# Key groups of one PSUM bank, query units over half a run, transposing transfers for four batches, and a new order of work

## The chip, the cores and the metric

The kernel runs on one core of one Trainium2 chip. The core has a matrix engine (TensorE, PE in the profile, with its weight loads listed as PEld), a vector engine (VectorE, DVE), an activation engine (ScalarE, ACT), a general engine (GpSimd, POOL) and a queue engine that mostly issues transfers (SyncE, SP). Each engine takes its instructions strictly in the order in which the program lists them; they meet only through semaphores. Matrix results land in PSUM, eight banks of 2 KB in each of 128 partitions, and everything else is in SBUF. The metric is device microseconds for one execution.

## The reference

Two layers for 8 batches of 576 tokens, 8 heads of 64: a linear attention with an exponential feature map, and behind it a causal gate of five taps around a linear unit.

```python
def phi(x):                                   # for q and for k
    proj = np.einsum('bhsd,df->bhsf', x, w_phi)          # 64 -> 128 features
    proj = proj - np.max(np.abs(proj), axis=-1, keepdims=True)
    return np.concatenate([np.exp(proj), np.exp(-proj)], axis=-1)
q_p, k_p = (phi(q), phi(k))
kv = np.einsum('bhsf,bhsd->bhfd', k_p, v)
z = np.sum(k_p, axis=2)
num = np.einsum('bhsf,bhfd->bhsd', q_p, kv)
den = np.einsum('bhsf,bhf->bhs', q_p, z)[..., None] + 1e-06
x = num / den                                 # heads joined: (8, 576, 512)
gate_pre[:, t] = sum(conv_w[m] * x[:, t - 4 + m] for m in range(5))
gate = 1.0 / (1.0 + np.exp(-gate_pre))
out = (gate * (x @ w_val)) @ w_out
```

The output is float32, 8 x 576 x 512. (The gate is computed as a tanh, with the halves folded into the taps and into the last scaling.)

## The kernel before

The eight batches run through one software pipeline. A batch has two tokens side by side in the 128 partitions (64 channels each), which gives 18 blocks of 128 columns; these are cut into five units (`UNITS`, four of four blocks and one of two).

For each batch, in the names that the code gives its tasks:

- **Loads.** k and q come from DRAM; for batch 0 as float32 in pieces on SP's queue (`load32`), turned by PE (`tp32`) and copied to bf16 by ACT or DVE (`tc32`); for batch 1 as bf16 by POOL's queue, turned by PE (`tp16`, `tc16`); from batch 2 on by POOL's queue and then turned by a transposing transfer on SP's queue (`xpose`). v comes in with `loadv`.
- **Keys.** `kp`: PE projects a unit into two banks, one for each of the two tokens. `kmax`: DVE takes the greatest magnitude over features out of both banks in one reduction. `kexp`: ACT takes the exponential of both banks, once for each sign. `ek` (ACT) makes the factors that undo the missing subtraction (exp of minus the maximum for one sign, of plus the maximum for the other), `vs` (POOL) multiplies them into v (tile VT), `st` (PE) sums keys times values, and `kv` (DVE or ACT) takes the sums out of PSUM.
- **Queries.** `qm`, `qmax`: the same projection and reduction. The maxima are turned (`mqt`, `mqr`) and spread over a diagonal by POOL (`rx`, tile RX); `qp` projects again in the other layout and subtracts the maxima by a second pair of matmuls against RX; `qexp` (ACT) writes the features into QTIL and, for the unit of two blocks, into QTT.
- **Attention out.** `num` (PE, five parts c = 0..4) waits in this version for every `qexp` of the batch; `nrm` (DVE) divides; the result is turned by PE and taken out of PSUM by DVE or ACT (`xtp`, `xtc`), or, for the batches in `XB`, turned by a transposing transfer on SP's queue (`xtd`).
- **Gate and output.** `gate` and `val` (PE), `tanh` (ACT), `gv` (DVE), `out` (PE), `oev` (ACT or DVE), and `odma`, the store on SP's queue.

The order of the work is written out in three tables. `build()` makes one list of tasks; `ORDER` is the sequence in which their instructions are put out, so that each engine's queue is the part of this sequence that belongs to it. `FLEX` gives an engine to each task that may run on two, and `BANKS` gives every group its PSUM banks. `WARM` and `ZERO` put further matmuls between the tasks, which add zeros to a bank (line 504) or are overwritten (line 491); the output doesn't depend on them. `hold` and `holdx` are tiny POOL copies that read a tile only so that POOL's queue of loads stands still until the tile has landed.

Of the kernel before, what the change touches and what calls it, by code (L numbers as in the profile page):

```python
# [27 lines left out]
XB = (6, 7)  # L28
# [6 lines left out]
WARM = (  # L35
    "60:6:1 81:1:1 87:7:2 134:7:1 141:7:1 "
)
ZERO = "35:76:7 61:80:5 75:34:1 101:105:1 118:99:1 126:215:8 144:223:1 155:192:4 158:200:1 175:315:6 189:346:1 195:241:2 197:241:2 211:327:1"
# [41 lines left out]
)  # L80
FLEX = (
    "AAAAAADAAADDPPPPDDDDAADDDDDDDDDDDDDAAADAAAADDDDAAADDDAADAAADDADAADDDDADDDDADDDDDDAADADDAAAAAA"
)
BANKS = (
    "037362307001454523232323016701676714232367230101676012354423010145454501013660564675601456745010145450101676767014501454"
# [77 lines left out]
def build(plan, em=None):  # L163
# [11 lines left out]
    def G(*k):  # L175
        return h.get(k)
# [724 lines left out]
```

## Time and profile before

| what | value |
|---|---|
| three timed runs | 218.59, 218.91, 219.14 us; median 218.91 us |
| span of the profiled execution, first to last instruction | 217.7 us |
| around the span (median less span; the page has no separate time for the profiled execution) | 1.2 us |
| PE busy | 195.5 us, 90% |
| ACT busy | 180.8 us, 83% |
| DVE busy | 170.2 us, 78% |
| POOL busy | 132.8 us, 61% |
| moved by DMA | 39.92 MB, 183 GB/s over the span |
| granted PE clock, mean | 0.995 |

The share of busy time of an engine is an average over the whole span, and this span has three parts: a start in which batch 0 has nothing beside it, a middle in which three batches overlap, and an end in which only the last gates and outputs are left. The table of stretches tells them apart. A row of instruction groups gives the busy time of the group, the mean of one instruction and the idle time in front of it; since consecutive instructions on ACT and DVE overlap by about a tenth of a microsecond, the busy time of a pair in the timeline is less than two means. PE's ends are modelled, and a matmul that waits inside the pipeline counts as busy.

### The profile page before, as it was taken

To read this page: it belongs to the slowest core of one execution; us is meant where nothing else is said; L and a number is where in the kernel's file an instruction comes from. 1 tells how busy PE (TensorE), PEld (TensorE's weight loads), DVE (VectorE), ACT (ScalarE), POOL (GpSimd) and SP (SyncE) were. 2 spreads that over 40 slices of the span, in tenths; PEclk is the share of its full clock that TensorE was granted. 3 is DMA by queue.
4 is the path that set the end of the run, shared out by engine and by line. 5 is a ranking of instruction groups with operands and counts; after the bars stand their busy time and mean duration, and the time that the engine had idled before them with its cause. 6 is when DMAs were issued, how large, how long until landed. Compare 5 with 4: busy or idle time off the path is not lost.

```text
span 217.7 us, 9029 instructions
## 1 busy us (share of the span) xinstructions
PE 195.5 (90%) x3946; PEld 138.6 (64%) x3946; DVE 170.2 (78%) x257; ACT 180.8 (83%) x267; POOL 132.8 (61%) x172
## 2 busy tenths in 40 slices
PE   2787887778999999998999999999999999899990
PEld 2555565566676676676857776567757766687740
DVE  3199979999789988997899978998699897654510
ACT  3589999999989899998999997999988988634251
POOL 3055999897793838970999089902993879210010
PEclk9999999999999999999999999999999999999997
DMA  6999998899899799989999778969953265764166
GB/s 177 364 234 215 302 188 231 149 174 199 144 152 284 139 135 213 302 154 174 233 276 168 88 165 248 190 142 203 287 183 89 63 160 128 81 168 97 48 186 202
DMA packets 49954, 39.92 MB, mean 183 GB/s; under 512 B 34165, under 2 KB 39541, under 8 KB 49914
## 3 DMA queue, kind: packets, MB, share of 16 engines
q1 hardware_dynamic: 43616, 28.65, 55.6%
q0 software_dynamic: 6032, 10.49, 26.3%
q8 instruction: 31, 0.51, 0.9%
q10 hardware_dynamic: 266, 0.21, 0.3%
q14 instruction: 9, 0.07, 0.1%
HBM read 30.48 MB, written 9.44 MB: 183 GB/s over the span
## 4 chain that ended last, share of the span: by engine, by line
PE 52%; ACT 23%; DVE 14%; DMA 5%; issue 4%; SPq 0%; DVEq 0%; ACTq 0%
PE PS L791 11%; ACT QTIL L706 9%; PE PS L781 9%; PE PS L813 9%; ACT KTIL L595 8%; DVE MQP L585 5%; PE PS L620 5%; PE PS L577 4%; PE PS L719 4%; DVE MK L585 3%; DMA KTIL<-in_k_dram 3%; PE PS L693 2%; DMA XT<-XN 2%; PE PS L817 2%; PE PS L698 2%
## 5 line engine op out<-in xcount | busy, mean ns | idle before, releaser
L595 ACT ACTIVATE KTIL<-PS 128x1024 bf16<-128x1024 f32 (+1 forms) x80 | 71.9, 960 | 4.1 <-PE PS L577 2.0
L610 POOL TENSOR_TENSOR VT<-VN,EK 128x1152 bf16<-128x1152 f32 x32 | 67.9, 2123 | 4.0 <-ACT EK L604 3.9
L706 ACT ACTIVATE QTIL<-PS 128x1024 bf16<-128x1024 f32 x64 | 62.5, 1044 | 2.4 <-PE PS L698 1.6
L682 POOL TENSOR_TENSOR RX<-MQR,ident 128x512 bf16<-128x512 bf16 (+1 forms) x39 | 36.6, 964 | 35.7 <-DVE MQR L670 26.0
L585 DVE TENSOR_REDUCE MK<-PS 128x8 f32<-128x1024 f32 (+1 forms) x40 | 44.2, 1112 | 2.9 <-PE PS L577 1.2
L585 DVE TENSOR_REDUCE MQP<-PS 128x8 bf16<-128x1024 f32 (+1 forms) x40 | 43.6, 1112 | 3.1 <-PE PS L577 2.3
L791 PE MATMUL PS<-XT,WV 128*128 128x288 bf16 x256 | 34.8, 286 | 0.3 <-DVE GV L797 0.2
L797 DVE SCALAR_TENSOR_TENSOR GV<-TH,PS 128x576 bf16<-128x576 bf16 x32 | 23.8, 752 | 10.4 <-PE PS L791 4.7
L813 PE MATMUL PS<-WOUT,GV 128*128 128x512 bf16 x128 | 31.3, 380 | 0.0
L791 PEld LDWEIGHTS <-WV 128*128 128x128 bf16 x256 | 23.8, 98 | 7.9 <-issue 1.4
L785 ACT ACTIVATE TH<-PS 128x576 bf16<-128x576 f32 x32 | 20.3, 663 | 9.5 <-PE PS L781 6.3
L620 PE MATMUL PS<-VT,KTIL 64*128 64x65 bf16 x1152 | 23.3, 191 | 1.1 <-issue 1.0
L781 PE MATMUL PS<-XT,GW 64*64 64x288 bf16 x640 | 23.1, 285 | 0.9 <-DMA XT<-XN 0.8
L740 DVE TENSOR_TENSOR XN<-PS,RCP 128x512 bf16<-128x512 f32 x32 | 22.1, 692 | 1.5 <-DMA XT<-XN 0.4
L620 PEld LDWEIGHTS <-KTIL 64*128 64x128 bf16 x1152 | 20.8, 94 | 3.8 <-issue 2.5
L719 PEld LDWEIGHTS <-QTIL 128*128 128x128 bf16 x512 | 18.3, 97 | 6.4 <-issue 4.0
L719 PE MATMUL PS<-KV,QTIL 128*128 128x65 bf16 x512 | 20.3, 194 | 0.3 <-DVE MQP L585 0.2
L781 PEld LDWEIGHTS <-GW 64*64 64x64 bf16 x640 | 17.8, 106 | 3.3 <-DVE RCP L737 0.9
L634 ACT ACTIVATE OUTS<-PS 128x512 f32<-128x512 f32 x22 | 13.5, 619 | 7.3 <-PE PS L813 6.1
L577 PE MATMUL PS<-W,qT 64*128 64x128 bf16 x288 | 15.1, 217 | 3.7 <-ACT qT L544 0.9
L813 PEld LDWEIGHTS <-GV 128*128 128x128 bf16 x128 | 11.1, 98 | 11.3 <-issue 0.6
L577 PEld LDWEIGHTS <-qT 64*128 64x128 bf16 x288 | 10.6, 94 | 10.3 <-issue 5.2
(79 smaller groups left out, 235.6 us busy)
## 6 DMA issues: line engine op xcount, KB each, us to landing
out_dram<-OUTS SPq DMA_DIRECT2D x32, 256.0 KB, 3.4
VN<-in_v_dram SPq DMA_DIRECT2D x7, 1152.0 KB, 6.3
KQN<-in_q_dram POOLq DMA_DIRECT2D x6, 576.0 KB, 8.3
KQN<-in_k_dram POOLq DMA_DIRECT2D x6, 576.0 KB, 9.8
KTIL<-in_k_dram SPq DMA_DIRECT2D x4, 288.0 KB, 4.5
VN<-in_v_dram POOLq DMA_DIRECT2D x1, 1152.0 KB, 10.6
KTIL<-in_q_dram SPq DMA_DIRECT2D x4, 256.0 KB, 5.7
out_dram<-OUTS SPq DMA_DIRECT2D x14, 64.0 KB, 2.6
```

The source lines that it names most:

```text
L577: nc.tensor.matmul(self.PS[:, t.grp.banks[par], i * P:(i + 1) * P], X[rows, (c0 + i) * P:(c0 + i + 1) * P], self.W2[rows, :], start=True, ...
L585: self.nc.vector.tensor_reduce(o, self.two(t.grp, n * P).rearrange("p a (c f) -> p a c f", f=F), AX.X, ALU.max, apply_absolute_value=True)
L595: self.nc.scalar.activation(self.KTIL[b % 2][:, s, c0:c0 + n, :, :].rearrange("p c a f -> p a c f"), self.two(t.grp, n * P).rearrange("p a ...
L610: nc.gpsimd.tensor_tensor(self.VT[g][:, s, :, 0:D], self.VN[b % 2][:, NC * g:NC * g + NC, :], e.to_broadcast([P, NC, D]), ALU.mult)
L620: nc.tensor.matmul(self.PS[:, t.grp.banks[ab], (s * 2 + x) * E1:(s * 2 + x + 1) * E1], self.KTIL[b % 2][rows, s, J // 2, J % 2, :], self.V ...
L682: self.nc.gpsimd.tensor_tensor(o, *wide(self.MQR[self.mq(b, u)][:, :], self.ident2), ALU.mult)
L706: self.nc.scalar.activation(o, i, AF.Exp, scale=1.0 - 2.0 * s)
L719: nc.tensor.matmul(self.PS[:, t.grp.banks[h // 4], (h % 4) * E1:(h % 4 + 1) * E1], Q[:, s, c % 2, h, (c // 2) * P:(c // 2 + 1) * P], self. ...
L781: self.nc.tensor.matmul(self.PS[o * D:(o + 1) * D, t.grp.banks[par], 0:R], self.GW[r, jj, 4 - m, :], X[r, 4 * a + jj, :, HALO - 8 * s:HALO ...
L791: self.nc.tensor.matmul(self.PS[:, t.grp.banks[par], 0:R], self.WV[:, i, (2 * j + par) * D:(2 * j + par + 2) * D], X[:, 4 * par + i, :, HA ...
L797: nc.vector.scalar_tensor_tensor(out=self.GV[b % 3][:, j, :, :], in0=self.TH[j][:, :, :], scalar=1.0, in1=self.two(t.grp, R), op0=ALU.add, ...
L813: nc.tensor.matmul(self.PS[:, t.grp.banks[0], :], GV[:, j, c % 2, (c // 2) * XH:(c // 2) * XH + P], self.WOUT[:, j, c % 2, :], start=(j == ...
```

## The change

Six things change, and the three tables with them.

1. **Key units.** A key unit still has one projection, but its two banks are two groups of their own (`gs`), each with its own reduction (`kmax`, one bank) and its own two exponentials (`kexp`, one bank). On DVE 40 reductions become 80 of half the size, on ACT 80 exponentials become 160 of half the size.
2. **Query units.** Units 0 to 3 no longer hold four blocks of all 16 runs of 8 tokens, but half of them (`qys`, `k=2`): units 0 and 1 make up one half of the columns of QTIL, units 2 and 3 the other. `num` for c = 0, 1 waits for units 0 and 1 alone, c = 2, 3 for units 2 and 3, c = 4 for unit 4. The second operand of `qp` is now contiguous (`RX[u][rows, 0:w]`). A unit needs two blocks of the turned input (`QNEED`), and in batch 0, whose maxima are turned in two parts, units 0 and 2 follow the first and the others the second (`QOF`).
3. **Transposing transfers.** `XB` grows from batches 6, 7 to 4, 5, 6, 7: 32 PE transposes and four copies out of PSUM go, and four transposing transfers of 256 KB come in on SP's queue.
4. **Engines.** `vs` and `rx` may run on DVE as well as on POOL. In the table, one of 32 `vs` and four of 40 `rx` are on DVE (one `rx` before). Of the copies, KV goes from 12 on DVE and 4 on ACT to 8 and 8, the output from 14 and 22 to 19 and 17.
5. **Filling matmuls.** `ZERO` is empty: the 152 matmuls against zeros go. `WARM` has one entry of two, against six matmuls in five entries.
6. **First loads.** The last piece of q is loaded first, `w_phi` comes in one transfer, `conv_w` moves from ACT's queue to SP's behind the pieces of k and q, and POOL's queue is held until all pieces of batch 0 have landed; batch 1 loads k ahead of q.

Of the order, three places. First SP's queue at the start of the program; KTIL_73 is the space into which the float32 pieces of batch 0 are loaded. Before:

```order
L527 DMA KTIL_73<-in_k_dram 128x576 x3
L525 DMA KTIL_73<-in_q_dram 128x512 x3
L527 DMA KTIL_73<-in_k_dram 128x576
L525 DMA KTIL_73<-in_q_dram 128x512
L525 DMA KTIL_73<-in_q_dram 128x256
L531 DMA VN_66<-in_v_dram 128x4x576
```

and after:

```order
L537 DMA KTIL_73<-in_q_dram 128x256
L539 DMA KTIL_73<-in_k_dram 128x576 x3
L537 DMA KTIL_73<-in_q_dram 128x512 x2
L539 DMA KTIL_73<-in_k_dram 128x576
L537 DMA KTIL_73<-in_q_dram 128x512 x2
L468 DMA cw_141<-in_moe_conv_w_dram 5x512
L543 DMA VN_66<-in_v_dram 128x4x576
```

The piece of 128 KB that was last is first, and a small transfer stands ahead of v.

Second, ACT's queue at the start (kT_68 and qT_70 are the turned keys and queries of batch 0, KTIL_72 its key features). Before:

```order
L454 DMA W_126<-in_w_phi_dram 64x128 x2
L456 DMA cw_141<-in_moe_conv_w_dram 5x512
L544 ACT_TABLE_LOAD
L544 CAST kT_68<-PS 128x512 x3
L595 ACTIVATE KTIL_72<-PS 128x2x4x128 x2
L544 CAST qT_70<-PS 128x512
L595 ACTIVATE KTIL_72<-PS 128x2x4x128
L544 CAST kT_68<-PS 128x512
```

and after:

```order
L464 DMA W_126<-in_w_phi_dram 128x1x128
L556 ACT_TABLE_LOAD
L556 CAST qT_70<-PS 128x256
L556 CAST kT_68<-PS 128x512 x2
L613 ACTIVATE KTIL_72<-PS 128x4x128 x9
L556 CAST qT_70<-PS 128x512
L613 ACTIVATE KTIL_72<-PS 128x4x128
L556 CAST kT_68<-PS 128x512
```

The first exponential stood behind three copies of keys and now stands behind two and a short one of queries; the exponentials have one bank each. On PE, in the same place, twelve float32 transposes stood ahead of the first projection, and now ten, two of them of queries.

Third, SP's queue where the result of batch 4 is ready (XN_97 and XN_98 hold it, XT_100 receives it turned; kT_69 and qT_71 are the turned inputs of batch 7). Before:

```order
L531 DMA VN_66<-in_v_dram 128x4x576
L830 DMA out_dram<-OUTS_112 16x8x512
L565 DMA_TRANSPOSE kT_69<-KQN_64 128x18x128
L565 DMA_TRANSPOSE qT_71<-KQN_65 128x18x128
L830 DMA out_dram<-OUTS_118 16x8x512
L830 DMA out_dram<-OUTS_117 16x8x512
```

and after:

```order
L857 DMA out_dram<-OUTS_116 16x8x512
L857 DMA out_dram<-OUTS_118 16x8x512
L782 DMA_TRANSPOSE XT_100<-XN_97 128x8x128
L782 DMA_TRANSPOSE XT_100<-XN_98 128x8x128
L577 DMA_TRANSPOSE kT_69<-KQN_64 128x18x128
L857 DMA out_dram<-OUTS_112 16x8x512
L577 DMA_TRANSPOSE qT_71<-KQN_65 128x18x128
```

The two transfers of the result stand ahead of the keys of batch 7 in the queue.

At the end of PE's queue, after the last `st`, stand in either version the rest of `num`, the gates and values of batches 6 and 7 and the outputs. Behind that point there were 36 `out` matmuls of full height (line 813) and 8 of half height (line 817), and there are now 44 and 16; the last store is now one of 256 KB, where it was four pieces of 64 KB.

```diff
-XB = (6, 7)
+QOF = {(0, 1): (0, 2), (2, 3, 4): (1, 3, 4), (0, 1, 2, 3, 4): (0, 1, 2, 3, 4)}
+QNEED = ((0, 1), (2, 3), (0, 1), (2, 3), (4,))
+XB = (4, 5, 6, 7)
-WARM = (
-    "60:6:1 81:1:1 87:7:2 134:7:1 141:7:1 "
-)
-ZERO = "35:76:7 61:80:5 75:34:1 101:105:1 118:99:1 126:215:8 144:223:1 155:192:4 158:200:1 175:315:6 189:346:1 195:241:2 197:241:2 211:327:1"
+WARM = "94:1:2"
+ZERO = ""
 ORDER = (
-    "1 2 9 3 4 11 5 6 10 21 22 19 20 13 12 46 25 26 7 8 23 24 14 27 28 42 29 32 30 33 44 49 76 31 15 43 45 47 16 158 159 48 "
+    "27 28 1 2 3 4 5 6 21 22 19 20 7 38 8 23 24 25 39 26 193 9 194 0 40 41 11 10 97 12 42 98 49 47 43 13 55 50 48 53 32 44 "
...
-                    hold = [None, A("lk", b, 0, "POOL", 0.15, fn("hold", HOLDU), [lds[HOLDU]], rank=-600)]
+                    hold = [None, A("lk", b, 0, "POOL", 0.15, fn("hold", HOLDU), lds + klds, rank=-600)]
...
-            g = plan.group("kp", 2)
-            kp = h["kp", b, u] = A("kp", b, u, "PE", 0.057 * n, fn("kp", b, u), [G("xk", b, u)], g, 1)
-            h["kmax", b, u] = A("kmax", b, u, "DVE", dve(2 * n * P, 0.08), fn("kmax", b, u), [kp, G("ek", b - 2)], g)
-            for s in range(2):
-                h["kexp", b, u, s] = A("kexp", b, u, "ACT", act(2 * n * P), fn("kexp", b, u, s),
...
+            gs = [plan.group("kp", 1) for _ in range(2)]
+            kp = h["kp", b, u] = A("kp", b, u, "PE", 0.057 * n, fn("kp", b, u), [G("xk", b, u)], gs[0], 1, also=gs[1])
+            for a in range(2):
+                h["kmax", b, u, a] = A("kmax", b, u, "DVE", dve(n * P, 0.08), fn("kmax", b, u, a), [kp, G("ek", b - 2)], gs[a])
+                for s in range(2):
+                    h["kexp", b, u, s, a] = A("kexp", b, u, "ACT", act(n * P), fn("kexp", b, u, s, a),
...
-                h["vs", b, gi, s] = A("vs", b, gi, "POOL", 2.22, fn("vs", b, gi, s),
+                h["vs", b, gi, s] = A("vs", b, gi, ("POOL", "DVE"), (2.22, 1.36), fn("vs", b, gi, s),
...
-        allq = [G("qexp", b, u, s) for u in range(NU) for s in range(2)] + [G("kv", b, i) for i in range(2)]
...
+            need = [G("qexp", b, u, s) for u in ((2 * (c // 2), 2 * (c // 2) + 1) if c < 4 else (4,)) for s in range(2)]
...
-        for i in range(2):
-            nc.scalar.dma_start(self.W32[i * D:(i + 1) * D, :], self.wphi[:, :])
+        nc.scalar.dma_start(self.W32[:, :], self.wphi[:, :].unsqueeze(0).to_broadcast([2, D, F]))
...
+    def kps(self, t, n):
+        return self.PS[:, t.grp.banks[0], 0:n * P].rearrange("p (c f) -> p c f", f=F)
+
+    def kmax(self, t, b, u, a):
+        c0, n = UNITS[u]
+        self.nc.vector.tensor_reduce(self.MK[b % 2][:, c0:c0 + n, a], self.kps(t, n), AX.X, ALU.max, apply_absolute_value=True)
+
+    def kexp(self, t, b, u, s, a):
+        c0, n = UNITS[u]
+        self.nc.scalar.activation(self.KTIL[b % 2][:, s, c0:c0 + n, a, :], self.kps(t, n), AF.Exp, scale=1.0 - 2.0 * s)
...
+    def qys(self, u):
+        return (8 * (u % 2), 8) if u < 4 else UNITS[4]
...
     def qp(self, t, b, u):
+            m = X[rows, y0 * P:(y0 + ny) * P]
+            m = m.rearrange("p (y h k x) -> p h k y x", y=ny, h=H, k=2)[:, :, u // 2] if u < 4 else m.rearrange("p (y h x) -> p h y x", y=ny, h=2 * H)
+            nc.tensor.matmul(self.PS[:, t.grp.banks[par], 0:w], self.W2[rows, :], m,
                              start=True, stop=True, skip_group_check=True)
...
+            nc.tensor.matmul(self.PS[:, t.grp.banks[par], 0:w], self.ONES[rows, 0:F], self.RX[u][rows, 0:w],
+                             start=False, stop=True, skip_group_check=True)
```

More of the change, by code (lines that the diff above doesn't have):

```diff
@@ L256, in build @@
         ld = h["lv0",] = A("lv", b, 0, "POOL" if b == 1 else "SP", 0.65, fn("loadv", b),
-               [G("vs", b - 2, g, s) for g in range(2) for s in range(2)] + [G("lv0",) if b > 2 else None],
+               [G("vs", b - 2, g, s) for g in range(2) for s in range(2)] + [G("lv0",) if b > 2 else hold[1] if b == 1 else None],
                rank=-980 if b == 0 else None)
@@ L298, in build @@
             mqr = A("mqr", b, i, "DVE", dve(128), fn("mqr", b, i), [mqt] + [G("rx", b - 2, u) for u in range(NU)], gm)
-            for u in us:
+            for u in QOF[us]:
                 n = UNITS[u][1]
-                h["rx", b, u] = A("rx", b, u, ("POOL", "DVE") if b == 0 else "POOL", (0.35 * n - 0.1, dve(n * P)) if b == 0 else 0.35 * n - 0.1,
+                h["rx", b, u] = A("rx", b, u, ("POOL", "DVE"), (0.35 * n - 0.1, dve(n * P)),
                                   fn("rx", b, u, i), [mqr, G("qp", b - 1, u)], gm if b == 0 else None)
@@ L503, in zero @@
                 rows = slice(par * D, (par + 1) * D)
-                self.nc.tensor.matmul(self.PS[:, t.grp.banks[par], c:w], self.NIL[rows, :], self.ONES[rows, c:w],
+                self.nc.tensor.matmul(self.PS[:, self.bank(t, par), c:w], self.NIL[rows, :], self.ONES[rows, c:w],
                                       start=False, stop=True, skip_group_check=True)
     def hold(self, t, u):
-        c = UNITS[u][0] * P
-        self.nc.gpsimd.tensor_copy(self.HOLD[:, :], self.XN32["q"][:, c:c + 1])
+        x = self.KTIL[1][:, :, :, :, :].rearrange("p s c a f -> p s (c a f)").bitcast(FP32)
+        self.nc.gpsimd.tensor_copy(self.HOLD[:, :, :], x.rearrange("p s (u x) -> p s u x", x=256)[:, :, :, 0])
     def holdx(self, t, b):
-        self.nc.gpsimd.tensor_copy(self.HOLD[:, :], self.XT_["q"][b % 2][:, NR - 1:NR])
+        self.nc.gpsimd.tensor_copy(self.HOLD[:, 0, 0:1], self.XT_["q"][b % 2][:, NR - 1:NR])
     def rows(self, w, b):
@@ L697, in qp @@
             rows = slice(par * D, (par + 1) * D)
[L698 to L699 removed]
+            nc.tensor.matmul(self.PS[:, t.grp.banks[par], 0:w], self.ONES[rows, 0:F], self.RX[u][rows, 0:w],
+                             start=False, stop=True, skip_group_check=True)
     def qexp(self, t, b, u, s):
         c0, n = UNITS[u]
[L703 removed]
         if u < 4:
[L705 to L706 removed]
+            self.nc.scalar.activation(self.QTIL[b % 2][:, s, :, :, u * D:(u + 1) * D],
+                                      self.two(t.grp, n * P).rearrange("p a (h r) -> p a h r", h=H), AF.Exp, scale=1.0 - 2.0 * s)
         else:
+            i = self.two(t.grp, n * P).rearrange("p a (h r) -> p a h r", h=2 * H)
             for a in range(2):
```

86 lines of the change are left out of this document (44 added, 42 removed), and 75 rows, old and new, of the table ORDER.

## The prediction

> **What bounds the kernel now.** I read the page first, its table of busy time and the slices:
>
> ```profile
> PE 195.5 (90%) x3946; PEld 138.6 (64%) x3946; DVE 170.2 (78%) x257; ACT 180.8 (83%) x267; POOL 132.8 (61%) x172
> PE   2787887778999999998999999999999999899990
> DVE  3199979999789988997899978998699897654510
> ACT  3589999999989899998999997999988988634251
> PEclk9999999999999999999999999999999999999997
> ```
>
> Four engines are busy, and none idles in plain sight; which of them sets the pace must be read by stretch. The columns are the stretch, its length, then busy time and count of PE, PEld, DVE, ACT, POOL, the granted clock, the DMA share and GB/s:
>
> ```profile
> 0.00:10.00 10.00, 4.93 (x32) 3.83 (x33) 2.00 (x6) 3.83 (x5) 1.78 (x12) 1.00 0.82 258
> 10.00:20.00 10.00, 7.73 (x122) 5.60 (x121) 9.32 (x10) 9.34 (x15) 5.68 (x8) 1.00 1.08 244
> 20.00:30.00 10.00, 8.39 (x136) 5.49 (x137) 8.45 (x15) 9.28 (x18) 8.13 (x7) 1.00 1.09 244
> 30.00:40.00 10.00, 8.45 (x272) 6.57 (x271) 9.57 (x12) 9.60 (x13) 9.19 (x12) 1.00 0.93 214
> 40.00:50.00 10.00, 7.38 (x202) 5.88 (x197) 8.94 (x16) 9.78 (x13) 9.97 (x10) 1.00 0.96 166
> 50.00:60.00 10.00, 9.28 (x225) 6.42 (x223) 8.46 (x12) 9.46 (x16) 7.12 (x10) 1.00 0.95 170
> 60.00:100.00 40.00, 38.10 (x833) 27.41 (x833) 35.26 (x54) 38.76 (x55) 27.77 (x35) 1.00 0.95 196
> 100.00:140.00 40.00, 39.64 (x822) 28.15 (x811) 36.27 (x56) 36.53 (x58) 30.36 (x37) 1.00 0.92 193
> 140.00:180.00 40.00, 39.86 (x773) 27.20 (x772) 35.41 (x52) 36.58 (x52) 25.07 (x33) 1.00 0.68 164
> 180.00:210.00 30.00, 29.23 (x550) 21.21 (x551) 16.56 (x32) 15.36 (x26) 7.73 (x14) 1.00 0.51 105
> 210.00:217.70 7.70, 2.52 (x16) 0.86 (x13) 0.00 (x0) 2.24 (x4) 0.00 (x0) 0.85 0.70 220
> ```
>
> So there are three regimes. From 10 to 60 us ACT sets the pace (47.5 us of 50), while PE has 8.8 us free and spends part of its busy time on matmuls against zeros. From 60 to 180 us PE does (117.6 of 120, and 79.5 of 80 in its last two rows), with ACT 8.1 us and DVE 13.1 us free. From 180 us on PE works nearly alone. Work taken from PE therefore pays behind 60 us, and work added to ACT costs ahead of it.
>
> When ACT gets its first real work is in the timeline (start, duration, instruction, idle time before it and who ended it):
>
> ```profile
> 3.85 2.23 PE L536 MATMUL PS<-ident_f,KTIL 128*128 128x128 f32 x9 [3.85 <-DMA KTIL<-in_k_dram]
> 7.29 0.90 PE L536 MATMUL PS<-ident_f,KTIL 128*128 128x128 f32 x3 [1.21 <-DMA KTIL<-in_k_dram]
> 8.13 1.04 PE L577 MATMUL PS<-W,kT 64*128 64x128 bf16 x16
> 8.23 0.59 ACT L544 CAST kT<-PS 128x512 bf16<-128x512 f32 x1 [1.74 <-PE PS L536]
> 9.21 1.94 ACT L595 ACTIVATE KTIL<-PS 128x1024 bf16<-128x1024 f32 x2 [0.39 <-PE PS L577]
> 10.32 0.69 DVE L542 CAST qT<-PS 128x512 bf16<-128x512 f32 x1 [4.80 <-ACT KTIL L595]
> ```
>
> The first projection stands on PE behind twelve transposes, the last of which wait for the third key piece until 7.29; nine are done at 6.08.
>
> **The change, step by step.** Durations, by shape (busy time, mean of one, idle before):
>
> ```profile
> L595 ACT ACTIVATE KTIL<-PS 128x1024 bf16<-128x1024 f32 x64 | 63.5, 1050 | 2.6 <-DVE MK L585 1.3 <-PE PS L577 0.6 <-DVE GV L797 0.3
> L595 ACT ACTIVATE KTIL<-PS 128x512 bf16<-128x512 f32 x16 | 8.8, 602 | 1.5 <-PE PS L577 1.3
> L709 ACT ACTIVATE QTT<-PS 128x256 bf16<-128x256 f32 x32 | 10.0, 421 | 1.5 <-PE PS L698 1.3
> L585 DVE TENSOR_REDUCE MK<-PS 128x8 f32<-128x1024 f32 x32 | 38.9, 1219 | 2.3 <-PE PS L577 1.2 <-ACT KTIL L595 0.7 <-ACT KV L632 0.2
> L585 DVE TENSOR_REDUCE MK<-PS 128x4 f32<-128x512 f32 x8 | 5.5, 686 | 0.7 <-ACT KTIL L595 0.3 <-PE PS L504 0.3
> L504 PE MATMUL PS<-ONES,NIL 64*128 64x128 bf16 x140 | 5.6, 216 | 0.0
> ```
>
> and consecutive ones, which overlap:
>
> ```profile
> 18.49 1.09 ACT L595 ACTIVATE KTIL<-PS 128x512 bf16<-128x512 f32 x2
> 23.68 1.21 ACT L709 ACTIVATE QTT<-PS 128x256 bf16<-128x256 f32 x4
> 10.93 2.35 DVE L585 TENSOR_REDUCE MK<-PS 128x8 f32<-128x1024 f32 x2
> ```
>
> *Key units on ACT.* In a row, one more exponential costs 1.94 - 1.05 = 0.89 us for two banks, 1.09 - 0.60 = 0.49 for 512 columns and (1.21 - 0.42) / 3 = 0.26 for 256. A batch has eight large ones (each becomes two of 512: +0.09) and two small ones (+0.03): +0.8 us, +6 us in all. Without overlap, by the means, it would be +0.15 and +0.24, so 64 x 0.15 + 16 x 0.24 = +13.5 us. I take 6, since ACT works back to back where it counts. Other copies leave ACT (five outputs, two XT, two casts) or come to it (four KV): about 3.4 us less, worked out in the same way from rows of 0.4 to 1 us. ACT's net is about +2.7 us. In the start (two and a half batches) it is 2.5 x 0.8 less 0.8 for two casts of batch 0: **+1.2 us**, on the pace-setting engine. Bounds: 0, if the 2.5 us that ACT idles there take it up, and +3.5 by the means. In the middle the rest lies in ACT's 8.1 free us: nothing, while that cover holds; gone, it costs the 1.5 us left.
>
> *Key units on DVE.* 32 x (2 x 0.60 - 1.13) plus eight small ones at about +0.06 is +2.7 us (+6 by the means). The other moves add about 3.6 us (five outputs, two casts, three more `rx`, one `vs`, less four KV and two XT). No row shows `vs` on DVE; 1152 elements at the slope of the reductions, (1219 - 686) / 512 ns each, make 1.2 us, POOL's 2.1 is the other end, 1.5 is taken. In all +6.3 us, under DVE's 13.1 free us of the middle: nothing. If DVE were to set the pace there it would be some 4 us. POOL loses about 5 us and waits less than before.
>
> *First loads.* Two key pieces are enough for the first projection now. The nine transposes that ended at 6.08 hold those of units 0 and 1; with the copy of 0.59 the projection could start at 6.7 and not at 8.13: -1.5 us. The 128 KB piece of q ahead of the keys costs 0.5 us at 258 GB/s, and its two transposes and projection 0.1 beside the wait. **-0.9 us**, between 0 (the keys land as late) and -1.5. ACT being the bound, this carries to 60 us. POOL's queue now has a GW of batch 0 ahead of its first `rx`, waiting for `conv_w` and DVE's cwP; `rx` and then `vs` are queued behind it, but they wait for maxima that DVE has later: nothing. The hold on all pieces waits for the same last landing as before.
>
> *PE.* 150 zero matmuls of line 504, two of line 497 and four of line 491 go, all in the first 50 us beside PE's own idle time: nothing, as long as the clock stays. The 32 transposes lie behind 100 us, where PE is full:
>
> ```profile
> 95.91 0.89 PE PS L748 x16
> ...
> 154.72 3.05 PE PS L791 x24
> ...
> 185.71 4.54 DMA XT<-XN
> ...
> 190.38 2.03 PE PS L781 x60
> ```
>
> In the chain of waits sixteen took 0.89 us: **-1.8 us**; at worst 0, if another engine sets the pace there.
>
> *The four transfers.* The transfer of batch 6 took 4.54 us, and the gate waited for it:
>
> ```profile
> PE PS L781 <- DMA XT<-XN: 0.8, 1, 0.8
> DMA to landing us min/median/max: 3.1/3.8/4.5
> ```
>
> From the last `num` to the gate it now takes a division (about 0.9), the issue of one transfer behind the other (1.3) and 3.1 to 4.5 us: 5.3 to 6.7. What the new order puts between them on PE I priced by such chain rows: for batch 5 24 `val` (3.05), three query units (about 1.2), 24 projections (0.9) and four `out` (0.9), some 6 us; for batch 4 9 us, for batch 6 6.6 and for batch 7 5.9 us (before: 5.1 for batch 6). So waits of 0 to 0.8 us at 5 and 7, taken as 0.3 each, and batch 6's 0.8 goes: **-0.2 us**, from -0.8 to +2. On SP's queue the keys of batch 7 stand behind the transfers of batch 4; they are used 70 us later.
>
> *Query units.* The same numbers of matmuls, exponentials and bytes. `num` may start after four exponentials and not after ten; what that is worth has no row. It can't exceed PE's idle time in the middle, 2.4 us, and it costs nothing: 0 taken.
>
> *The end.* PE's last matmul ends at 212.5, 5.2 us ahead of the end:
>
> ```profile
> 211.47 1.05 PE L817 MATMUL PS<-WOUT,GVT 128*64 128x512 bf16 x8
> out_dram<-OUTS SPq DMA_DIRECT2D x32, 256.0 KB, 3.4
> out_dram<-OUTS SPq DMA_DIRECT2D x14, 64.0 KB, 2.6
> ```
>
> The last store is now a 256 KB one, without a second issue of 0.6 ahead of it: **+0.3 us** (0 to +0.8). The eight full and eight half-height `out` more behind the last `st` are work that PE has to do in any case.
>
> The sum is -0.9 + 1.2 - 1.8 - 0.2 + 0.3 = -1.4 us: a span of 216.3. With the 1.2 us around the span that separate 217.7 from the median of 218.91, the forecast is **217.5 us**.
>
> [...]
>
> **The rivals.**
>
> *ACT pays for the halves.* If ACT sets the pace beyond 60 us too, its whole net of 2.7 us lands on the end, PE's 1.8 doesn't count, and the earlier start is used up by the denser queues: 218.9 + 2.7 = 221.6. For it: 38.8 of 40 us busy from 60 to 100. Against it: 36.5 of 40 from 100 on. It decides once ACT is over 97% busy behind 100 us. [...]
>
> *The clock falls.* Without the zeros PE's own work is about 6 of 10 us from 10 to 50. If the granted clock halved for one such stretch, 6 us become 12, 2 over its length; for one and a half stretches, 217.5 + 3 = 220.5. Against it: 4.93 of 10 us busy from 0 to 10 went with a clock of 1.00; only behind the last matmul is there a row of 0.85. [...]
>
> *The transfers come late.* DMA is at a share of 0.92 from 100 to 140, where batches 4 and 5 would have theirs; those measured ran at 0.51. At twice the duration each of two gates waits 3 to 4 us more, half of it under work put between: 217.5 + 3 = 220.5.
>
> *The finer pieces close the gaps.* ACT's idle 2.5 us from 10 to 60 and PE's 2.4 in the middle are waits for whole banks and whole batches. Half of them gone: 217.5 - 2.5 = 215.0; all: 212.6.
>
> *Nothing comes of it.* Gain and added ACT work cancel: 218.9.
>
> **How the numbers follow.** A measurement of this kernel tells about 0.3% (0.7 us) from no change. The forecast, 216 to 218.2, has 0.41; closed gaps 0.19; nothing 0.08; ACT 0.18; the clock 0.06; late transfers 0.08. So faster 0.60, same 0.08, slower 0.32. The range reaches from 213.8, half way between the two closings, to ACT's 221.6; what lies outside is under 2 in 10. The likeliest case alone ranges from 216 to 218.2.
>
> **What would show it.** ACT's first key exponential near 8.3 instead of 9.21; its busy time near 183.5 and DVE's near 176; no row of line 504's kind; PE still at over 99% from 100 to 180; a wait of the gate for XT's transfer under 1 us at each batch; clock 1.00 up to 210. I am wrong if ACT's busy time is over 190, if PE falls below 97% in the middle, if the first exponential is no earlier, or if the gates of batches 4 and 5 stand waiting.

## The result: slower, and the profile after

The changed kernel takes 231.62 us in the median (230.12 to 234.50) and the kernel before 218.88 us: a ratio of 1.0561, with a 95% interval of 1.0508 to 1.0614, or +12.3 us. (Differences in us follow from the ratios, which leave out runs more than 1.5% above the fastest of their kernel; so they are not quite the differences of the medians.) The forecast was 217.5 us in a range of 213.8 to 221.6; both the size and the sign were wrong. The profiled execution took 231.72 us with a span of 229.9.

The page of the changed kernel, its busy times and slices:

```profile
PE 195.3 (85%) x3740; PEld 134.7 (59%) x3758; DVE 177.2 (77%) x304; ACT 181.5 (79%) x341; POOL 130.8 (57%) x167
PE   1887677699899949999999989969969998999990
ACT  2699999989999946999989979969778899453321
PEclk9999958979999979999999999999999999999997
```

The busy times are near the forecast (ACT 181.5 for 183.5, DVE 177.2 for 176): the work is what was counted. What is new is empty slices in the middle of PE's row and notches in its clock. By stretch, with the columns of the prediction's table (50 to 60 and the end left out):

```profile
10.00:20.00 10.00, 8.16 (x91) 5.13 (x91) 9.91 (x16) 10.00 (x22) 7.06 (x9) 1.00 1.02 237
20.00:30.00 10.00, 6.89 (x104) 4.54 (x103) 9.23 (x17) 10.00 (x22) 9.63 (x9) 0.95 1.10 247
30.00:40.00 10.00, 7.94 (x234) 6.80 (x233) 9.15 (x19) 9.52 (x21) 9.86 (x13) 0.70 0.93 137
40.00:50.00 10.00, 7.78 (x166) 5.91 (x163) 8.17 (x15) 9.54 (x18) 9.37 (x10) 0.83 1.12 189
60.00:100.00 40.00, 34.27 (x658) 23.50 (x659) 32.13 (x53) 33.22 (x64) 26.84 (x33) 0.96 0.91 197
100.00:140.00 40.00, 38.19 (x790) 25.72 (x787) 36.43 (x66) 37.44 (x76) 27.69 (x35) 1.00 0.95 192
140.00:180.00 40.00, 34.48 (x654) 22.94 (x656) 31.06 (x50) 33.43 (x62) 15.91 (x21) 1.00 0.92 181
```

From 60 to 180 us PE is busy for 34.27 + 38.19 + 34.48 = 106.9 of 120 us, where it was 117.6: about 10.7 us of the 12.3, and 89% busy where the prediction called itself wrong under 97%. ACT falls idle with it there (33.2 of 40 where it had 38.8), so ACT is not what holds PE up. Four rows of PE's waits name what does:

```profile
PE PS L636 <- issue: 5.3, 2, 3.5
PE PS L589 <- DVE MQP L600: 2.8, 6, 0.9
PE PS L808 <- DMA XT<-XN: 2.2, 1, 2.2
PE PS L589 <- DMA qT<-KQN: 0.8, 1, 0.8
```

"Issue" is time in which PE waited for nothing that the profile shows. PE's and SP's timelines show the longest of them:

```profile
79.60 0.39 PE L636 MATMUL PS<-VT,KTIL 64*128 64x65 bf16 x14
83.46 0.64 PE L636 MATMUL PS<-VT,KTIL 64*128 64x65 bf16 x22 [3.47 <-issue]
```

```profile
73.36 0.54 SPq L543 DMA_DIRECT2D VN<-in_v_dram  x1
74.01 6.96 SPq L577 DMA_TRANSPOSE kT<-KQN  x1
81.07 4.00 SPq L577 DMA_TRANSPOSE qT<-KQN  x1
```

PE stops in the middle of a row of 36 equal matmuls, and the profile shows nothing that it waits for. On SP the key transpose of batch 4 stands right behind a load of v and takes 6.96 us; in the kernel before, where that load is issued elsewhere, it took 2.80:

```profile
76.38 2.80 SPq L565 DMA_TRANSPOSE kT<-KQN  x1
```

The DMA views of the two transposes' first microseconds (74 to 79 us after, 76 to 79 us before) show that the late one had moved almost nothing. The packets of the transposes are those under 512 bytes: in the second view the key transpose is the one transfer issued, and 1145 of 1146 packets are that small.

```profile
DMA packets 607, 1.28 MB, mean 256 GB/s; under 512 B 32, under 2 KB 32, under 8 KB 607
...
kT<-KQN SPq DMA_TRANSPOSE x1
```

```profile
DMA packets 1146, 0.31 MB, mean 103 GB/s; under 512 B 1145, under 2 KB 1145, under 8 KB 1145
...
kT<-KQN SPq DMA_TRANSPOSE x1, 6.4
```

The page has a queue q8 that it calls instruction, with 29 packets after and 31 before, each of 16 KB (0.48 and 0.51 MB in all). I take them for pieces of PE's instructions, because of when they come: counted in the trace, a piece started every 254 executed PE instructions (matmuls and weight loads) in the median of the kernel before and after 383 at the most. In the changed kernel the one at 80.78 came 521 instructions after the last, and the one at 150.02 after 437. These are the two places where PE stood for 3.47 and 1.88 us, and PE went on 1.61 and 1.23 us after the piece's packet had ended (81.85 and 151.12). The kernel before has such a stop too, of 0.96 us at 98.0, with a piece from 96.76 to 97.72 and PE going on 1.28 us later; what is new is the length. These three are all the stops of 0.8 us and more that the two profiles put down to "issue". So I read the two long ones as a chain, a load, a transpose behind it, the fetch of a piece behind that and PE behind the fetch, that no row of the page shows in one piece.

The notches in the clock: the granted clock was 0.50 from 29.1 to 35.9, 46.2 to 49.6 and 83.7 to 87.1. The windows ahead of and behind each fall:

```profile
25.70:29.10 3.40, 1.95 (x40) 1.14 (x35) 3.29 (x5) 3.40 (x6) 3.40 (x5) 1.00 1.24 348
29.10:32.50 3.40, 1.76 (x38) 1.36 (x39) 3.19 (x6) 3.40 (x10) 3.40 (x3) 0.50 1.16 186
42.80:46.20 3.40, 1.87 (x32) 1.17 (x31) 3.05 (x5) 3.40 (x9) 3.40 (x6) 0.99 1.14 211
46.20:49.60 3.40, 3.40 (x88) 2.92 (x87) 1.99 (x4) 3.34 (x6) 3.40 (x5) 0.50 1.03 164
80.30:83.70 3.40, 0.24 (x15) 0.24 (x16) 0.26 (x1) 1.80 (x3) 2.65 (x4) 1.00 1.18 144
83.70:87.10 3.40, 3.07 (x27) 1.73 (x21) 1.99 (x3) 1.08 (x2) 0.00 (x0) 0.50 1.02 204
```

Ahead of the first two PE was busy for 1.95 and 1.87 of 3.4 us, with no gap over 0.73 and 1.39 us; the third follows the 3.47 us in which PE stood. In all some 13.6 us ran at half speed, which is 6.8 us of PE's full-speed time (a fall behind the last matmul, as in the kernel before, is not counted).

Where the loss builds up is seen from when every 32nd `val` matmul ended, that is, one batch's worth (the last column is the kernel of the first experiment):

```
batch   before   after     after, v behind
0        67.1     +1.1        +0.7
1        87.2     +7.5        +3.0
2       114.0     +7.7        +3.3
4       157.8    +12.7        +8.1
5       174.0     +9.3        +3.0
7       205.5    +12.9        +6.7
```

At the end of the start the changed kernel is 1.1 us behind, little for 10.2 us at half speed; it loses 6.4 us where the load of v meets the transpose of batch 4, and 5.2 us more by the end of batch 4.

### The profile page after: what moved, and what is told of

Same layout as the page of the kernel before. It is cut to its first block, busy times and chain, and to the rows that moved or that the text cites. A ratio compares the mean times of both kernels' runs of the same rounds, so it can differ in the third digit from the quotient of the medians.

```text
span 229.9 us, 8751 instructions
## 1 busy us (share of the span) xinstructions
PE 195.3 (85%) x3740; PEld 134.7 (59%) x3758; DVE 177.2 (77%) x304; ACT 181.5 (79%) x341; POOL 130.8 (57%) x167
## 4 chain that ended last, share of the span: by engine, by line
PE 49%; DVE 19%; ACT 11%; DMA 9%; issue 6%; POOL 3%; SPq 0%; ACTq 0%; DVEq 0%
PE PS L818 9%; PE PS L636 9%; DVE MQP L600 8%; PE PS L840 7%; PE PS L808 7%; ACT KTIL L613 6%; PE PS L589 4%; DVE MK L609 3%; PE PS L746 3%; DMA qT<-KQN 3%; DMA XT<-XN 3%; POOL VT L626 3%; DVE XN L767 2%; ACT QTIL L731 2%; DMA KTIL<-in_k_dram 2%
## 5 line engine op out<-in xcount | busy, mean ns | idle before, releaser
L613 ACT ACTIVATE KTIL<-PS 128x512 bf16<-128x512 f32 (+1 forms) x160 | 81.2, 596 | 6.2 <-DVE MK L609 3.7
L626 POOL TENSOR_TENSOR VT<-VN,EK 128x1152 bf16<-128x1152 f32 x31 | 65.7, 2119 | 20.7 <-ACT EK L619 16.8
L731 ACT ACTIVATE QTIL<-PS 128x1024 bf16<-128x1024 f32 x64 | 65.0, 1065 | 5.8 <-PE PS L725 5.4
L600 DVE TENSOR_REDUCE MQP<-PS 128x8 bf16<-128x1024 f32 (+1 forms) x40 | 43.7, 1111 | 10.9 <-PE PS L589 10.5
L609 DVE TENSOR_REDUCE MK<-PS 128x4 f32<-128x512 f32 (+1 forms) x80 | 48.3, 627 | 2.5 <-ACT KTIL L613 1.4
L701 POOL TENSOR_TENSOR RX<-MQR,ident 128x512 bf16<-128x512 bf16 (+1 forms) x36 | 34.7, 988 | 19.1 <-DVE MQR L686 17.1
L636 PE MATMUL PS<-VT,KTIL 64*128 64x65 bf16 x1152 | 24.8, 199 | 7.0 <-issue 5.3
L636 PEld LDWEIGHTS <-KTIL 64*128 64x128 bf16 x1152 | 22.6, 100 | 9.9 <-issue 6.0
L650 ACT ACTIVATE OUTS<-PS 128x512 f32<-128x512 f32 x17 | 10.0, 606 | 15.2 <-PE PS L840 6.6
L589 PE MATMUL PS<-W,kT 64*128 64x128 bf16 x288 | 16.4, 232 | 3.5 <-DVE MQP L600 2.1
L646 DVE TENSOR_SCALAR OUTS<-PS 128x512 f32<-128x512 f32 x19 | 13.1, 687 | 7.1 <-PE PS L840 3.7
```

What stands on the lines that cost most here:

```text
L600: self.nc.vector.tensor_reduce(o, self.two(t.grp, n * P).rearrange("p a (c f) -> p a c f", f=F), AX.X, ALU.max, apply_absolute_value=True)
L609: self.nc.vector.tensor_reduce(self.MK[b % 2][:, c0:c0 + n, a], self.kps(t, n), AX.X, ALU.max, apply_absolute_value=True)
L613: self.nc.scalar.activation(self.KTIL[b % 2][:, s, c0:c0 + n, a, :], self.kps(t, n), AF.Exp, scale=1.0 - 2.0 * s)
L626: eng.tensor_tensor(self.VT[g][:, s, :, 0:D], self.VN[b % 2][:, NC * g:NC * g + NC, :], e.to_broadcast([P, NC, D]), ALU.mult)
L636: nc.tensor.matmul(self.PS[:, t.grp.banks[ab], (s * 2 + x) * E1:(s * 2 + x + 1) * E1], self.KTIL[b % 2][rows, s, J // 2, J % 2, :], self.V ...
L701: self.nc.gpsimd.tensor_tensor(o, *wide(self.MQR[mq][:, :], self.ident2), ALU.mult)
```

## The experiments

Theories after this reading: *collision* (a transposing transfer issued while a bulk load runs waits for it and holds back PE's instructions; the new order of loads and the four new transfers bring this about), *clock* (without fillers PE's clock halves), *late transfers*, and, as rivals, *ACT pays for the halves* and *PE's order as such*. Six kernels edit the changed one, and six put parts of the change into the kernel before. The kernel before ran on the same chip each time; differences are to it.

**The loads of v behind the transposes** (the changed kernel; SP's order):

```diff
-loadv 3
 xpose k4
 xpose q4
+loadv 3
-loadv 5
-loadv 6
 xpose q6
+loadv 5
+loadv 6
```

> The changed kernel with three loads of v (batches 3, 5 and 6) issued on SP's queue behind the q transpose that they stood ahead of. Theory 'collision': the load ahead stretched the transpose of batch 4 to 7.0 us, held back the fetch of PE's instructions (80.78) and so starved PE for 3.47 us, which then halved the clock for 3.4 us: the stall near 80 us and the half-speed stretch at 83.7 are gone, 231.6 - 5.2 = about 226.4 us. Rival 'clock and transfers': the loads' place is of no account, the stall comes again, 231.6 +- 1 us.

227.80 us, ratio 1.0391 (1.0287 to 1.0494): +8.5 us where the changed kernel has +12.3. SP and PE at the place:

```profile
73.15 3.83 SPq L578 DMA_TRANSPOSE kT<-KQN  x1
78.30 2.81 SPq L578 DMA_TRANSPOSE qT<-KQN  x1
81.22 1.10 SPq L544 DMA_DIRECT2D VN<-in_v_dram  x2
```

```profile
80.65 0.53 PE L637 MATMUL PS<-VT,KTIL 64*128 64x65 bf16 x22 [1.11 <-issue]
```

The transpose takes 3.83 us, PE stands 1.11 us instead of 3.47, and the half-speed stretch at 83.7 is gone, as the collision theory has it. The table above shows the gain at its place: +7.5 becomes +3.0. In the median the run gains 3.7 us and not the expected 5.2, and with both intervals the 3.7 is uncertain by some 2.5 either way. The profiled execution was the fastest of the four (225.59 us, 6.1 us under the profiled one of the changed kernel), so its trace can't show what the others lost. It does show a new loss: PE starved at another transpose, 2.52 us at 144.9 (1.88 at 150.5 in the changed kernel), with a half-speed stretch at 146.9. There the loads of q and k for batch 7 (135.6) run between the two transposing transfers of batch 4 and the key transpose.

**Fillers in free banks** (the changed kernel):

```diff
-WARM = "94:1:2"
+WARM = "94:1:2 140:5:2 144:2:2 148:4:2 152:3:3 155:6:3 162:7:3 168:3:3 ..."
```

> The changed kernel with 32 more filler matmuls of 512 columns (0.21 us each) in 13 places between 25 and 46 us, in banks that nothing uses there. Theory 'clock': the granted clock stays at 1.00 from 29 to 36 and from 46 to 50 us, where it fell to 0.5; 5.1 us of PE's time come back, half of them on the path: about 229 us. Rival 'ACT sets the pace of the start anyway': the clock stays up, but the time is the same within 1 us of 231.6, or later where the fillers delay PE.

239.12 us, ratio 1.0886 (1.0780 to 1.0991). Worse than either expectation.

```profile
PE 205.9 (87%) x3791; PEld 136.4 (57%) x3791; DVE 178.9 (75%) x304; ACT 182.8 (77%) x341; POOL 131.2 (55%) x167
```

PE's busy time rose by 10.6 us and its idle time from 10 to 60 us fell only from 10.4 to 7.7: the fillers stood in front of work that was ready. The clock did stay at 1.00 from 29 to 50 us, but fell at 20.7, before the first filler, and for 6.8 us each at 85.6 and 157.2, where PE stood for 3.63 and 3.62 us: more half speed in all than without the fillers. Two other executions, with a mean clock of 0.979 where the changed kernel's profile has 0.964, still took 237.31 and 238.46 us. So this run doesn't price the clock.

**The tokens of batches 4 and 5 back to PE** (the changed kernel):

```diff
-XB = (4, 5, 6, 7)
+XB = (6, 7)
```

with PE's transposes and the copies in the places of the transfers.

> The changed kernel with the four transposing transfers of batches 4 and 5 given back to PE (32 transposes, four copies). Theory 'late transfers': the wait of the gate near 170 (2.2 us), the wait behind the q transposes near 160 (0.8) and the starved stretch near 150 (1.9) go, 1.8 us of PE work come back: 231.6 - 3.1 = about 228.5 us. Rival 'PE is the bound': the 32 transposes only add, 233.4 us.

234.32 us, ratio 1.0706 (1.0620 to 1.0792): the rival's side. The profiled execution was the slowest of the four (236.74) and has half speed from 20.4, 30.7 and 85.3 us, the first two ahead of any place that was edited, so little is to be read from it beyond the sign.

**All three edits.**

> The three edits together. If the three losses are separate and are all there is: 231.6 - 5.2 - 2.5 - 3.1 = about 220.8 us, near the kernel before. If the new order or the halved key units cost something of their own, it stays above 224 us.

233.20 us, ratio 1.0658 (1.0579 to 1.0737), clock 0.993. Here the clock is nearly whole and the time isn't: 6.9 us of fillers (33 of 0.21) and 1.8 us of transposes were added to PE. It tells that the losses in this order can't be taken off one by one, and so the parts were taken to the order of before.

**The loads of v ahead of the transposes, in the kernel before.** The mirror image of the first run:

```diff
+loadv 4
 xpose k4
 xpose q4
-loadv 4
(the same for 5 and 6)
```

> The kernel before with three loads of v (batches 4, 5 and 6) moved on SP's queue from behind to right ahead of the key transpose of the same batch; nothing else. Theory 'collision' (a transposing transfer that is issued while a bulk load runs waits for it, and holds back the fetch of PE's instructions): the key transposes take some 7 us instead of 2.8, PE stands without an instruction for 1 to 3.5 us at one to three of the places, with a half-speed stretch of 3.4 us behind it: 218.9 + 3 to 10 us, 222 to 229. Rival 'order of PE's work': the loads' place costs nothing, 218.9 +- 0.7.

The four runs took 223.58 to 228.54 us, beside 217.83 to 220.11 for the kernel before. The two lowest, 223.58 and 225.17, are 5.1 and 6.7 us above its median of 218.51: the collision theory's side. SP and PE at the second place:

```profile
97.60 0.53 SPq L532 DMA_DIRECT2D VN<-in_v_dram  x1
100.26 5.26 SPq L566 DMA_TRANSPOSE kT<-KQN  x1
105.62 3.81 SPq L566 DMA_TRANSPOSE qT<-KQN  x1
```

```profile
109.67 0.61 PE L578 MATMUL PS<-W,kT 64*128 64x128 bf16 x8 [4.48 <-DMA kT<-KQN]
```

The transpose of batch 5 takes 5.26 us (3.58 before; at the other two places 5.83 and 5.94 for 2.80 and 2.84), its projection waits 4.48 us, and the clock halves from 109.1 to 112.5. At the third place PE starved for 1.33 us (126.1). No work was added or taken away, so the place of these loads alone costs 5 us and more in this order. The route was partly another one than I had expected: the plain wait for the keys was larger than the starved stretch.

**Four more transposing transfers, alone** (the kernel before, `XB = (4, 5, 6, 7)`, transfers in the places of PE's transposes):

> The kernel before with the tokens of batches 4 and 5 turned by transposing transfers as well, put where PE's transposes stood. By the prediction's terms: 32 transposes go (-1.8) and the waits at the gates are small: 217 us. Theory 'collision': the transfers of these two batches meet bulk loads of keys, queries or v, land 7 us and more after their issue instead of 3.8, and hold back PE's instructions: at least 2 us slower than before, 221 us or more.

223.50 us, ratio 1.0208 (1.0147 to 1.0268): +4.5 us (3.2 to 5.9).

```profile
135.37 6.41 SPq L756 DMA_TRANSPOSE XT<-XN  x2
```

```profile
148.62 0.65 PE L720 MATMUL PS<-KV,QTIL 128*128 128x65 bf16 x16 [1.31 <-DVE XN L741]
149.20 0.44 PE L727 MATMUL PS<-KV,QTT 128*64 128x65 bf16 x16
150.87 0.94 PE L782 MATMUL PS<-XT,GW 64*64 64x288 bf16 x12 [1.23 <-DMA XT<-XN]
```

The transfers of batch 4 (135.4) meet the loads of q and k for batch 7 (134.2 and 135.8) and SP needs 6.41 us for the two. They hold XN, which DVE wants to write again, so `num` waits 1.31 us; then the gate waits 1.23; behind this the clock is at half from 150.5 to 153.9 (1.7 us). That is 4.2 us, less 1.8 us of transposes that PE is spared; the profiled span grew by 4.7, so some 2 us of it I can't point to.

**Key units by single banks, alone** (the kernel before, same groups and places):

```diff
-        self.nc.scalar.activation(
-            self.KTIL[b % 2][:, s, c0:c0 + n, :, :].rearrange("p c a f -> p a c f"),
-            self.two(t.grp, n * P).rearrange("p a (c f) -> p a c f", f=F),
-            AF.Exp, scale=1.0 - 2.0 * s)
+        for a in range(2):
+            i = self.PS[:, t.grp.banks[a], 0:n * P].rearrange("p (c f) -> p c f", f=F)
+            self.nc.scalar.activation(self.KTIL[b % 2][:, s, c0:c0 + n, a, :], i, AF.Exp, scale=1.0 - 2.0 * s)
```

and so the maxima.

> The kernel before with each maximum and each exponential of a key unit issued as two, one for each of its banks, in the same groups and places. ACT's busy time rises by 6 us (6 by consecutive rows, 13 by the means). If only the start pays: 2.5 batches at 0.8, 218.9 + 2 = 220.9 us. If ACT pays throughout: 218.9 + 6 = 224.9 us. If it is hidden: 218.9.

219.55 us, ratio 1.0046 (1.0019 to 1.0072): +1.0 us.

```profile
PE 196.5 (90%) x3946; PEld 138.9 (64%) x3946; DVE 171.9 (79%) x297; ACT 184.6 (85%) x347; POOL 132.9 (61%) x172
```

ACT's busy time rose from 180.8 to 184.6, 48 ns for each of 80 exponentials, and DVE's by 1.7 us, 43 ns for each of 40 maxima. It lies between the case in which it is hidden (218.9) and the one in which only the start pays (220.9).

**No fillers, alone** (the kernel before):

```diff
-ZERO = "35:76:7 61:80:5 75:34:1 ..."
+ZERO = ""
-WARM = "60:6:1 81:1:1 87:7:2 134:7:1 141:7:1"
+WARM = "87:7:2"
```

> The kernel before without its 152 zero matmuls and without four of its six filler matmuls of line 491. The trace of before has its fillers in stretches of 3.4 us that end at 14.0, 17.4, 31.0 and 41.3 us, where PE without them is busy 0.51 to 0.59 of the time; the changed kernel's clock halved behind stretches at 0.58 and 0.54. Theory 'clock': one to three half-speed stretches before 60 us, 1 to 4 us slower, 220 to 223 us. Rival 'idle time only': clock 1.00, 218.9 +- 0.7.

221.17 us, ratio 1.0119 (1.0069 to 1.0170): +2.6 us (1.5 to 3.7). Windows ahead of and behind its two falls:

```profile
10.10:13.60 3.50, 2.09 (x30) 1.21 (x29) 3.50 (x4) 2.95 (x5) 2.88 (x5) 0.99 0.93 296
13.60:17.00 3.40, 2.94 (x21) 2.04 (x23) 2.85 (x5) 3.38 (x6) 0.00 (x0) 0.50 1.06 192
37.50:40.90 3.40, 1.65 (x28) 1.13 (x28) 3.37 (x6) 3.40 (x6) 2.18 (x4) 0.99 0.71 193
40.90:44.30 3.40, 3.12 (x42) 2.23 (x42) 3.10 (x4) 3.40 (x5) 3.39 (x5) 0.50 0.74 111
```

The falls come behind the stretches that end at 13.6 and 40.9, two of the four that were named from the trace of before. The first fall lasts to 23.8, so 13.6 us run at half speed in all, 6.8 us of PE's full-speed time, of which 2.6 reach the end. The fillers weren't idle decoration: with them, in the kernel before, the granted clock is 1.00 in every row of the prediction's table from 10 to 60 us.

**The loads of batch 7 out of the way** (the changed kernel with v behind; POOL's order):

```diff
-load q7
-load k7
 halo 4
 vs 5 0 0
+load q7
+load k7
 vs 5 0 1
```

> The changed kernel with the three loads of v behind the transposes, as in a_vn, and the loads of q and k of batch 7 moved on POOL's queue from ahead of the second transposing transfer of batch 4 to behind the v products that follow it, so that transfer and load no longer meet. All four transposing transfers stay. Theory 'collision': the starved stretch of 2.52 us near 145 and the half-speed stretch of 3.4 us behind it go: 227.8 - 4.2 = about 223.6 us. Rival 'the transfers as such': PE starves near 145 all the same, 227.8 +- 1.5.

232.34 us, ratio 1.0589 (1.0530 to 1.0649): a miss for both theories. PE starved 0.87 us near 145 instead of 2.52 (and stood 0.96 us at 143.8), the half-speed stretch behind it stayed (146.6 to 150.1), and SP's queue now stood at the key transpose until 150.6, output stores waited behind it, DVE found no free output buffer, and PE had no bank:

```profile
DVE OUTS L647 <- DMA out_dram<-OUTS: 3.9, 1, 3.9
```

```profile
158.06 0.37 PE L780 MATMUL PS<-ident,XNT 128*128 128x128 bf16 x2 [3.75 <-DVE OUTS L647]
```

The collision was traded for a jam on SP. The edit neither refutes the cause nor confirms it; it shows that the one other place tried for these loads isn't free.

**v behind, and the tokens back to PE** (the changed kernel):

> The changed kernel with the three loads of v behind the transposes, as in a_vn, and the transposes of batches 4 and 5 given back to PE; no fillers. Taken the other way on the kernel before, the four transfers cost 5.0 us. If that is their price here too: 227.8 - 5.0 = about 222.8 us. If in this order PE is late anyhow and the 32 transposes (1.8 us) only add, as they seemed to with the loads in the way: 228 to 230 us.

230.40 us, ratio 1.0505 (1.0453 to 1.0558), about 2.5 us above the run with v behind alone: near the second expectation. No token transfer stands in the way any more, but PE now waits where the new order has no room for copies:

```profile
PE PS L637 <- DVE VT L628: 1.6, 1, 1.6
PE PS L590 <- ACT XT L649: 1.5, 2, 0.9
PE PS L809 <- DVE XNT L768: 0.9, 1, 0.9
```

So the four transfers can't be priced by taking them out of an order that was made with them; in the order of before they cost 4.5 us.

**An earlier start, alone** (the kernel before):

```diff
 tp32 k0
 tp32 k1
-tp32 k2
 kp 0 1
 kp 0 0
+tp32 k2
```

and its copy behind ACT's first two exponentials.

> The kernel before with the transposes of the third key piece and their copy moved behind the first two projections on PE and the first two exponentials on ACT. The first two projections need only two key pieces, whose transposes end at 6.08; by the prediction's term for the first loads the first key exponential moves from 9.21 to some 8.0 us, and since ACT sets the pace up to 60 us, the end moves by -0.9 (0 to -1.2): 217.6 us. Rival 'PE catches up': the start's gain is used up by 60 us, 218.5 us.

218.95 us, ratio 0.9991 (0.9960 to 1.0022): no change. ACT's first exponential:

```profile
7.76 1.94 ACT L596 ACTIVATE KTIL<-PS 128x1024 bf16<-128x1024 f32 x2 [1.24 <-PE PS L578]
```

It begins 1.45 us earlier, and nothing of it arrives: the rival's case.

**Three parts at once** (the kernel before, its own order: four transfers, single-bank key units, no fillers):

> The kernel before, in its own order, with three of the change's parts at once: four more transposing transfers (alone +5.0 us), the key units' maxima and exponentials by single banks (alone +1.0), no fillers (alone +2.7). If the prices add up, 218.5 + 8.7 = about 227.2 us, and with the 3.8 us that the loads of v cost in the changed kernel that is 231.0 of its 231.6: the query units, the first loads and the rest of the new order then come to nothing together. If it stays under 225 us the parts share their losses, and the new order has a price of its own.

226.57 us, ratio 1.0331 (1.0247 to 1.0416): +7.2 us (5.4 to 9.1) for 4.5 + 1.0 + 2.6 = 8.1 alone. The prices nearly add up. With the 3.7 us that the loads of v cost in the changed kernel this is 10.9 of 12.3 us; the 1.4 us left lie within the intervals, which are wide (this run's alone is 3.7 us), and the prices come from two different orders. The half-run query units weren't tried by themselves: they and the rest of the order are in that remainder.

## Why the prediction was wrong, point by point

- **The four transfers, "-0.2 us, from -0.8 to +2"**, together with the 32 PE transposes at -1.8: this is the largest failure. Measured alone they come to +4.5 us. The step priced the new transfers by those of batch 6, which ran at a DMA share of 0.51 with no bulk load near; the median from issue to landing went from 3.8 to 7.0 us in the changed kernel, and in the run that has them alone SP took 6.41 us for the two of batch 4. The step saw the wait of the gate, but not that the transfer holds XN (1.31 us of wait in that run), nor the half-speed stretch that came behind the waits there (150.5 to 153.9), nor the starved PE (3.47 and 1.88 us in the changed kernel). The rival "late transfers" had the right reason and 0.08; at 220.5 it was also too cheap.
- **"On SP's queue the keys of batch 7 stand behind the transfers of batch 4"**: true and beside the point. The step looked at what stands behind the new transfers and not at what stands ahead of the old ones. That three loads of v had been moved ahead of the transposes (3.7 us by the first experiment) appears in no term. The rows were there: from 56 us on the kernel before issues each load of v behind a q transpose (63.25 behind 59.64, 83.57 behind 79.29), and its transposes when the loads of q and k have landed.
- **"nothing, as long as the clock stays" for the fillers**: the condition was the term. Alone +2.6 us. The rival "the clock falls" was priced at +3 over the forecast. It reckoned with 15 us at half speed, and there were 13.6, so its price was nearly right; but it was given 0.06, because I took the trace's shares over slices of 5.4 us and rows of 10 us, and took it that the clock would hold, which nothing showed: the row of 1.00 from 0 to 10 us lies ahead of the trace's first record of the clock, at 10.5 us. In the changed kernel the clock fell twice, at 29.1 and 46.2, behind 3.4 us in which PE was busy for 1.95 and 1.87 us, with no gap over 1.39 us. The half-speed stretches there, ahead of the last matmul, last 6.8, 3.4 and 3.4 us.
- **Key units on ACT, +1.2 us on the path**: the right place, half the size. The 1.2 were 2.0 for the key units less 0.8 for two casts; tried alone, without the casts and together with DVE's halves, the key units cost 1.0 (0.4 to 1.6) and not 2.0. The gross term of 6 us for ACT was 3.8. The run alone gives 48 ns for each exponential more and 43 ns for each maximum more. The rival "ACT pays for the halves" fell: ACT is busy for 37.4 and 33.4 of 40 us behind 100.
- **Key units on DVE, 0**: DVE's busy time came out as forecast (177.2 for 176) and nowhere sets PE's pace in the middle. At the projections PE now waits 2.8 us for DVE's maxima of q (the second row of its waits above), all of it before 53 us; how much of the start that costs was not told apart from ACT's part.
- **First loads, -0.9**: the first exponential came at 8.72 (forecast 8.3, before 9.21), and a start 1.45 us earlier brought nothing when tried alone. "ACT being the bound, this carries to 60 us" was the wrong step; the rest of the new loads (the order of q, the held queue) was not tried by itself.
- **The end, +0.3**: 5.2 us lie between PE's last matmul (224.7) and the end, as before. Nothing.
- **The range**: it was drawn from rivals that come one at a time. Three losses of 2.6, 3.7 and 4.5 us came together, all by the way of PE, which had 2.4 us of free time in 120 to lose.

## What to carry to other kernels

Where one engine is busy for 98% of a stretch, read a change from what can make that engine wait, and first from the queues: list for each transposing transfer which bulk loads run when it is issued, on any queue, before and after. Look at the clock before removing fillers from PE: here the kernel before ran at 1.00 up to its last matmul with them, and for 13.6 us at 0.50 without them. So compute PE's busy share without them over stretches as short as the falls (3.4 us here), wherever they may begin, not over ten. And price a part of a change in the old order as well as by its removal from the new one; the two answers differed here by 7 us for the same four transfers.

## What the runs showed of the hardware that I had not expected

- **The clock fell behind stretches with little work on PE, but not behind each of them.** I laid stretches of 3.41 us, the length of the shorter falls, over the two profiles of the kernels, from the first record of the clock (10.5 us before, 12.0 after) to the last matmul. In the changed kernel five at full clock have PE busy for less than 0.60: behind those that end at 29.1 (0.58), 46.2 (0.54) and 83.7 (0.07) the clock was 0.50, behind those that begin at 148.6 (0.56) and 169.0 (0.43) it stayed at 1.00. In the kernel before the lowest share is 0.63 (from 14.0) and the clock stayed at 1.00. Half speed went on behind one stretch of 0.52 (from 29.1) and ended behind three of 0.89, 1.00 and 0.90. The share is what my count of PE's rows gives; what else decides was not shown. Where the falls lie differs between profiles (29.1 and 27.5 us for the first one of the changed kernel and of the one with v behind, which are the same up to there).
- **Transposing transfers hardly moved while bulk loads ran.** In the changed kernel a transpose issued 0.65 us behind a load of 1152 KB had moved 32 packets 5 us later; in the kernel before, the same transpose, issued at 76.4 with no such load right ahead of it, had moved 1145 by 79. The same shows with a load on POOL's queue: beside the loads of q and k issued at 138.3 and 138.9 the two token transfers (256 KB each), issued from 138.7 on, had moved 31 packets under 512 bytes between 139.0 and 143.5, and 570 more from 144 to 148. The longest case in the changed kernel is the q transpose of batch 6, behind two loads of v: 8.30 us on SP at 126.3 (3.24 before), with 18 small packets by 131, and without a long stop of PE.
- **PE stopped where pieces of the instruction queue came late.** In the changed kernel it stopped for 3.47 and 1.88 us at the pieces that came 521 and 437 instructions after the last. That the meeting of load and transpose causes the first, and doesn't merely coincide with it, rests on the moved loads: with them out of the way 3.47 us became 1.11. Which of the two transfers holds the pieces back was not told apart, and not every late piece was followed by a stop: in the kernel before one came 383 instructions after the last, at 138.93, its longest distance, and PE made no stop of 0.8 us there.
